# Scores and y on four 64x64 quadrants of TensorE, with keys and values put in order by their casts

## The chip, the cores and the metric

The kernel runs on one core of a Trainium2 chip. The metric is the device time of one execution in microseconds (us). Engines are named as the profile names them: PE is TensorE (PEld its weight loads), DVE is VectorE, ACT is ScalarE, POOL is GpSimd, SP is SyncE, whose queue issues most of the DMAs.

## The reference

Attention over 4 batches, 8 heads, 768 positions and head size 64, with 4 sink keys and a causal window of 128, followed by a feed-forward layer with a maximum of three products:

```python
scores = scale * np.matmul(q, k.transpose(0, 1, 3, 2))
rel = pos[:, None] - pos[None, :]
keep = (pos[None, :] < 4) | ((rel >= 0) & (rel < 128))
a = softmax(np.where(keep, scores, -1e9))            # over the keys
x = np.matmul(a, v)                                  # to (3072, 512)
h = np.maximum(np.maximum(x @ w1, x @ w2), x @ w3)   # (3072, 768)
out = h @ w_out                                      # (3072, 512), float32
```

## The kernel before

The 3072 positions are cut into 12 chunks of 256, three to a batch. Matrices are bf16, sums are float32 in PSUM. A chunk passes these steps:

- `load` brings q, k and v (512 KB each) in through SP's queue, into two buffers each. Row p of a tile holds positions 2p and 2p + 1, so that 512 bytes lie together.
- `cast_qk` (L95) and `cast_v` (L104) turn float32 into bf16. For q and k there are two casts per chunk, of 128 rows by 512 values. For v there are four, of 64 rows by 512, since they also move the rows to their places. After chunk 4, `cast` (L475) gives all of them to POOL, in the order k, q, v.
- Q and k are transposed: chunks 0 to 3 on PE (`turn`, L109), later ones by DMA (`turn_dma`, L150). Q takes one transfer, k takes two of 64 rows.
- `score` (L259) works head pair by head pair, four pairs to a chunk. The stationary operand is 64 partitions (the head's size) by 128 keys, and the two heads of a pair sit in the two row halves of the array. Keys and queries come in blocks of 128. A chunk with a predecessor in its batch has three steps: the previous chunk's last key block against the first query block, the chunk's first key block against both, its last key block against the second. These are 128, 256 and 128 columns. The first chunk of a batch (0, 3, 6, 9) has only the last two.
- `expo` on ACT takes the exponential, `mask` (L289) on DVE multiplies by a mask of ones and zeros (chunks 0 and part of 1 add theirs on PE first).
- `sink_score` (L294) gets the scores of the 4 sink keys for the second and third chunk of a batch. It reads `ks`, which `sink_k` (L224) copies on POOL out of the batch's first `kT`.
- `av_open` and `av` (L324, L339) multiply by v and divide by the sum of the weights, `xpose_dma` transposes the result.
- `ffn_h` (L383) makes h: 72 matmuls of 256 columns per chunk, a copy on ACT and two maxima on DVE for every two blocks.
- Y = h times w_out is made by `ffn_y` with full weights, or by `y_open`, `y_turn` and `y_out` (L428, the loop L431) in row halves: two turns of 12 matmuls of 512 columns, with the halves of a wave writing to different banks of PSUM. After the first turn a matmul of one column, the fence, is put in; its bank is given to the next score.

The order is written out by hand. Up to chunk 3 it is a list of calls (L486 to L692). Then a loop (L693) runs rounds: round i makes the scores, the weights and the A·V of chunk i + 1, h of chunk i and y of chunk i - 1, loads chunk i + 3, and casts and transposes chunk i + 2. Rounds 3, 10 and 11 have an order of their own, rounds 4 to 9 another. Every engine, and SP's queue, runs its instructions in the order of this list, so a waiting one holds up all behind it. Banks of PSUM are handed out in the order in which they are given back.

In the list, POOL's work ahead of the scores of chunk 4 is: mask factors (L592), casts of v of chunk 2, of q and k of chunk 3, three of v of chunk 3 (L651 to L654), one of k of chunk 4 (L659), four of v of chunk 4 (L662, L689 to L691), and then `sink_k` at the head of round 3.

Of the kernel before, what the change touches and what calls it, by code (L numbers as in the profile page):

```python
# [16 lines left out]
def kernel(  # L17
# [31 lines left out]
    with tc.manual_schedule():  # L49
# [16 lines left out]

        RING = 4
# [6 lines left out]
        raws, bfs = {}, {}  # L74

# [28 lines left out]
        def cast_v(ci, n, i, eng):  # L104
            eng.tensor_copy(  # L105
                vb[ci % RING][64 * i:64 * i + 64, n, :, 0:D],
                raws[ci, "v"][64 * n:64 * n + 64, :, i])

        def turn(ci, w, g, eng=None):  # L109
# [8 lines left out]
            if w == "q":  # L118
                f(  # L119
                    qT[ci % RING][:, 2 * g:2 * g + 2].rearrange("q p i n r -> q (p i) (n r)"), pt)  # L120
            else:
                f(
                    kT[ci % RING][:, :, 2 * g:2 * g + 2].rearrange("q n p i r -> q n (p i) r"),
                    pt.rearrange("q x (n r) -> q n x r", r=64))
# [25 lines left out]
        def turn_dma(ci, w):  # L150
            if ci >= NCH:
                return
            if w == "q":
                nc.sync.dma_start_transpose(
                    out=qT[ci % RING].rearrange("q p i n r -> q (p i) (n r)"),
                    in_=bfs[ci, w].rearrange("s p i a d -> s (p i a d)"))
                return
            for n in range(2):
                nc.sync.dma_start_transpose(
                    out=kT[ci % RING][:, n].rearrange("q p i r -> q (p i) r"),  # L160
                    in_=bfs[ci, w][64 * n:64 * n + 64].rearrange("q p i a d -> q (p i a d)"))


# [25 lines left out]
        msk0 = const.tile([128, 2, 3, 128], BF16, name="msk0")  # L189

# [20 lines left out]

        sel = const.tile([128, 2, 32], BF16, name="sel")

# [10 lines left out]
        def sink_k(b):  # L224
            x = kT[(b * CPB) % RING]
            for a in range(2):
# [3 lines left out]
                    x[hp, 0, :, :, 0:2].rearrange("q p i r -> q p r i"))  # L230
# [28 lines left out]
        def score(ci, pairs):  # L259
            b, c = divmod(ci, CPB)  # L260
# [20 lines left out]

        def expo(ci, p):
            lo = 0 if ci % CPB else 1
# [5 lines left out]
        def mask(ci, p, eng=None):  # L289
            lo = 0 if ci % CPB else 1  # L290
# [3 lines left out]
        def sink_score(ci):  # L294
# [4 lines left out]
            for p in range(NP):  # L299
                nc.tensor.matmul(  # L300
                    st[32 * p:32 * p + 32].rearrange("q n (i r) -> q n i r", i=2),
                    lhsT=ks[b % 2][:, p],
                    rhs=qT[ci % RING][:, p].rearrange("q i n r -> q n i r"),
# [6 lines left out]
        def sink_v(b):  # L310
# [3 lines left out]
            for a in range(2):  # L314
                for p in range(NP):
                    nc.tensor.matmul(
                        sv[32 * p:32 * p + 32, a], lhsT=sel[:, a], rhs=x[:, 0, 2 * p + a],
# [21 lines left out]
        def av(ci, p):  # L339
# [16 lines left out]
            if ci not in xs:  # L356
                xs[ci] = work.tile([128, 2, NP, 2, D], BF16, tag="x", bufs=2, name="x_sb")
            nc.vector.tensor_mul(xs[ci][:, :, p], o[:, :, :, 0:D],  # L358
# [5 lines left out]
        def xpose(ci, t, eng=None):  # L364
            eng = eng or nc.scalar
            if t == 0:
                xTs[ci] = work.tile([128, 2, DS, 128], BF16, tag="xT", bufs=3, name="xT")
            pt = bank([128, DS, 128], BF16, "xt")
            x = xs[ci][:, t].rearrange("q p a d -> q (p a d)")
            for ds in range(DS):  # L370
                nc.tensor.transpose(pt[:, ds], x[:, ds * 128:(ds + 1) * 128], ident)
            (nc.scalar.copy if eng is nc.scalar else eng.tensor_copy)(xTs[ci][:, t], pt)
            give(pt)

        def xpose_dma(ci, eng=None):
            xTs[ci] = work.tile([128, 2, DS, 128], BF16, tag="xT", bufs=3, name="xT")
            (eng or nc.sync).dma_start_transpose(
                out=xTs[ci].rearrange("q t s r -> q (t s) r"),
                in_=xs[ci].rearrange("q t p a d -> q (t p a d)"))
# [3 lines left out]
        def ffn_h(ci, fp, wi, cuts=1, eng=nc.scalar):  # L383
# [3 lines left out]
            for f in range(2):  # L387
                c0 = (2 * fp + f) * 128
                for ds in range(DS):
                    nc.tensor.matmul(  # L390
                        hp[:, f].rearrange("q (i t r) -> q i t r", i=2, t=2),
                        lhsT=w_sb[wi][:, ds, c0:c0 + 128],
# [459 lines left out]
```

## Time and profile before

| | |
|---|---|
| median of 3 runs | 176.93 us (176.87 to 177.23) |
| the profiled execution, its own time | 178.83 us |
| its span, first to last instruction | 177.1 us |
| granted clock of TensorE, mean | 1.000 |
| busy: PE, weight loads, DVE | 167.9, 128.2, 121.7 us |
| busy: ACT, POOL | 86.8, 65.9 us |

The share of an engine is an average over the whole span. Where a stage's limit lies is read from that stage: the busy time of each engine within a stretch, the order of instructions in time, and the idle time ahead of an instruction with what ended it. A line such as "L105 POOL CAST vb<-v_raw 64x512 bf16<-64x512 f32 x4" says which line of the kernel the instruction comes from, its engine, what it writes and reads, the partitions by elements, and how many are merged. The duration of a matmul includes its way through the array, so the distance between starts is what it costs in a stream.

### The profile page before, as it was taken

What the parts mean: (1) busy time and instruction counts of PE and PEld (TensorE: products, weight loads), DVE (VectorE), ACT (ScalarE), POOL (GpSimd) and SP (SyncE); (2) the same over time, 40 slices, a digit from 0 to 9 for tenths busy, and PEclk for the clock granted to TensorE, in tenths of its full rate; (3) what the DMA queues carried; (4) which work ended last, traced back from release to release, by engine and by line L of the source; (5) the groups of instructions that cost most, each with busy time, mean ns of one, the idle gap of its engine ahead of it and who ended that gap; (6) DMA issues with size and microseconds to landing.
All of it is one profiled execution on the core that took longest, in us unless ns stands there. A gap on an engine that the chain in (4) does not pass through costs nothing.

```text
span 177.1 us, 4816 instructions
## 1 busy us (share of the span) xinstructions
PE 167.9 (95%) x1956; PEld 128.2 (72%) x1961; DVE 121.7 (69%) x263; ACT 86.8 (49%) x174; POOL 65.9 (37%) x126
## 2 busy tenths in 40 slices
PE   7869988899999999999999999999999999999992
PEld 2436777676688588598698797697797796796871
DVE  3287763679599696677776775876776776876451
ACT  4588525477871931931823914914715716420210
POOL 7289605454685296056055046065073000000000
PEclk9999999999999999999999999999999999999999
DMA  5999999999999999799998999997999405303203
GB/s 144 298 282 181 161 223 236 222 288 276 277 197 302 289 229 237 172 301 171 229 262 214 230 217 234 183 273 194 255 210 226 73 15 162 122 0 63 118 2 118
DMA packets 70694, 34.91 MB, mean 197 GB/s; under 512 B 26640, under 2 KB 69136, under 8 KB 70672
## 3 DMA queue, kind: packets, MB, share of 16 engines
q1 hardware_dynamic: 64976, 31.33, 79.4%
q0 software_dynamic: 5552, 3.15, 12.9%
q8 instruction: 15, 0.25, 0.6%
q10 hardware_dynamic: 144, 0.13, 0.2%
q14 instruction: 7, 0.06, 0.1%
HBM read 25.17 MB, written 6.29 MB: 178 GB/s over the span
## 4 chain that ended last, share of the span: by engine, by line
PE 75%; DMA 11%; POOL 6%; DVE 5%; issue 2%; POOLq 0%; SPq 0%; DVEq 0%
PE h_ps L390 44%; PE y_ps L431 10%; DMA q_raw<-in_q_dram 7%; PE y_ps L411 6%; PE st L274 5%; PE o L350 5%; DMA v_raw<-in_v_dram 3%; POOL w L237 3%; DVE h_sb L401 2%; POOL vb L105 1%; PE o L332 1%; DVE e_sb L292 1%; PE y_ps L453 1%; DVE x_sb L358 1%; PE pt L115 1%
## 5 line engine op out<-in xcount | busy, mean ns | idle before, releaser
L390 PE MATMUL h_ps<-xT,w 128*128 128x256 bf16 x864 | 101.6, 273 | 0.9 <-DMA w<-in_moe_w_dram 0.8
L390 PEld LDWEIGHTS <-w 128*128 128x128 bf16 x864 | 81.6, 98 | 11.8 <-DMA w<-in_moe_w_dram 1.2
L401 DVE TENSOR_TENSOR h_sb<-h_sb,h_ps 128x512 bf16<-128x512 bf16 (+1 forms) x74 | 49.1, 670 | 19.7 <-PE h_ps L390 18.0
L286 ACT ACTIVATE e_sb<-st 128x512 bf16<-128x512 f32 (+1 forms) x96 | 45.9, 585 | 6.6 <-PE st L274 6.5
L397 ACT CAST h_sb<-h_ps 128x512 bf16<-128x512 f32 x35 | 20.6, 589 | 49.7 <-PE h_ps L390 49.6
L292 DVE TENSOR_TENSOR e_sb<-e_sb,msk 128x1024 bf16<-128x1024 bf16 (+1 forms) x42 | 28.0, 679 | 10.8 <-ACT e_sb L286 10.8
L105 POOL CAST vb<-v_raw 64x512 bf16<-64x512 f32 x42 | 27.8, 661 | 15.7 <-DMA v_raw<-in_v_dram 13.2
L101 POOL CAST k_bf<-k_raw 128x512 bf16<-128x512 f32 x18 | 11.0, 630 | 40.0 <-DMA k_raw<-in_k_dram 32.8
L358 DVE TENSOR_TENSOR x_sb<-o,rc 128x256 bf16<-128x256 f32 x48 | 20.4, 424 | 1.6
L431 PE MATMUL y_ps<-wo,h_sb 64*128 64x512 bf16 x168 | 20.7, 376 | 0.0
L350 PE MATMUL o<-vb,e_sb 128*128 128x65 bf16 x352 | 16.6, 193 | 0.8 <-ACT e_sb L286 0.8
L350 PEld LDWEIGHTS <-e_sb 128*128 128x128 bf16 x352 | 14.6, 97 | 3.2 <-ACT e_sb L286 1.0
L274 PE MATMUL st<-qT,kT 64*128 64x128 bf16 (+1 forms) x256 | 14.8, 237 | 0.2 <-DVE qT L119 0.2
L101 POOL CAST q_bf<-q_raw 128x512 bf16<-128x512 f32 x17 | 10.2, 619 | 9.0 <-DMA q_raw<-in_q_dram 9.0
L274 PEld LDWEIGHTS <-kT 64*128 64x128 bf16 x256 | 9.2, 94 | 5.6 <-issue 1.8
L431 PEld LDWEIGHTS <-h_sb 64*128 64x128 bf16 x168 | 8.9, 94 | 5.7
L411 PE MATMUL y_ps<-wo,h_sb 128*128 128x512 bf16 x49 | 12.6, 380 | 0.3
L355 DVE RECIPROCAL rc<-o 128x4 f32<-128x4 f32 x48 | 8.4, 174 | 3.6 <-PE o L350 3.6
L306 ACT ACTIVATE e_sink<-sk 128x256 bf16<-128x256 f32 x8 | 3.1, 389 | 13.3 <-PE sk L300 13.3
L411 PEld LDWEIGHTS <-h_sb 128*128 128x128 bf16 x54 | 4.9, 98 | 5.4 <-DVE h_sb L401 0.5
L237 POOL DMA_DIRECT2D w<-in_moe_w_dram x9 | 7.1, 790 | 0.0
L445 DVE COPY y_sb<-y_ps 128x512 f32<-128x512 f32 x8 | 5.4, 686 | 0.8 <-PE y_ps L431 0.5
(73 smaller groups left out, 87.3 us busy)
## 6 DMA issues: line engine op xcount, KB each, us to landing
k_raw<-in_k_dram SPq DMA_DIRECT2D x11, 512.0 KB, 5.5
v_raw<-in_v_dram SPq DMA_DIRECT2D x11, 512.0 KB, 7.5
out_dram<-y_sb SPq DMA_DIRECT2D x11, 512.0 KB, 3.1
q_raw<-in_q_dram SPq DMA_DIRECT2D x10, 512.0 KB, 7.2
w<-in_moe_w_dram POOLq DMA_DIRECT2D x9, 256.0 KB, 6.8
q_raw<-in_q_dram SPq DMA_DIRECT2D x4, 256.0 KB, 8.5
wo<-in_moe_w_out_dram POOLq DMA_DIRECT2D x2, 384.0 KB, 8.2
v_raw<-in_v_dram SPq DMA_DIRECT2D x2, 256.0 KB, 5.9
```

What stands on the lines that cost most here:

```text
L101: f(x[:, 2 * g:2 * g + 2].rearrange("q p i a d -> q p a i d"), y[:, 4 * g:4 * g + 4].rearrange("q (p a) i d -> q p a i d", a=2))
L105: eng.tensor_copy(vb[ci % RING][64 * i:64 * i + 64, n, :, 0:D], raws[ci, "v"][64 * n:64 * n + 64, :, i])
L274: nc.tensor.matmul(st[a][:, s:s + q1 - q0].rearrange("q n (i r) -> q n i r", i=2), lhsT=x[hp, n, p].rearrange("q i r -> q (i r)"), rhs=qc[ ...
L286: nc.scalar.activation(e[:, a, lo:], st[a][:, lo:], AF.Exp, scale=scale)
L292: (eng or nc.vector).tensor_mul(e[:, :, lo:], e[:, :, lo:], msk0 if lo else msk)
L350: nc.tensor.matmul(o[:, t, a], lhsT=e[:, a, s], rhs=vb[cv % RING][:, n, 2 * p + a], start=first, stop=True, skip_group_check=True)
L358: nc.vector.tensor_mul(xs[ci][:, :, p], o[:, :, :, 0:D], rc.unsqueeze(3).to_broadcast([128, 2, 2, D]))
L390: nc.tensor.matmul(hp[:, f].rearrange("q (i t r) -> q i t r", i=2, t=2), lhsT=w_sb[wi][:, ds, c0:c0 + 128], rhs=xTs[ci][:, :, ds].rearrang ...
L397: (nc.scalar.copy if eng is nc.scalar else eng.tensor_copy)(dst, hp)
L401: nc.vector.tensor_max(dst[:, x], dst[:, x], hp[:, x])
L411: nc.tensor.matmul(yp, lhsT=hs[ci][:, fb, t * 128:(t + 1) * 128], rhs=wo[:, fb], start=(fb == 0), stop=(fb == FB - 1))
L431: nc.tensor.matmul(yps[ci][t], lhsT=hs[ci][hp, fb, t * 128:(t + 1) * 128], rhs=wo[hp, fb], start=(turn == 0 and fb == 0), stop=(turn == 1 ...
```

## The change

From chunk 3 on (`NEW = 3`):

- Scores (`score4`) and y use four quadrants of 64 rows by 64 columns. Keys are put in order so that a block of 64 holds consecutive positions. For a chunk with a predecessor, the quadrants that the mask makes all zero are left out, and the rest is ordered in three steps of equal length in the two column halves: 192, 128 and 64 columns. The first chunk of a batch keeps 256 and 128. A wave of y has four matmuls instead of two, 24 to a turn.
- The exponentials of such a chunk then have 384 columns instead of 512 (`expo4`); `mask4` reads them with an overlapping pattern and writes a tile of the old form.
- `cast_k` puts the keys in order with eight casts of 32 rows, `cast_v` the values likewise. K is transposed by one transfer.
- POOL casts q first, then k, then v. For chunk 4, DVE makes four of k's casts and POOL four. `masks2` (L592's place) and `masks3` build the new masks and a second selector on POOL.
- The A·V result and its transpose have their middle dimensions exchanged. H reads its columns in runs of 32.
- In rounds 4 to 9 the first turn of y comes after one pair of scores instead of two, in round 10 likewise, and the fence stands a pair of scores further ahead of the score that takes its bank. In round 3, q is transposed ahead of k.

```diff
+        def cast_k(ci, n, h, i, eng):
...
+            x, y = 64 * h + 32 * i, 64 * n + 32 * h
+            f = eng.copy if eng is nc.scalar else eng.tensor_copy
+            f(bfs[ci, "k"][x:x + 32, :, n],
+              raws[ci, "k"][y:y + 32, :, i].rearrange("q (p a) d -> q p a d", a=2))
...
+            for h in range(2):
+                x, y = 64 * h + 32 * i, 64 * n + 32 * h
+                eng.tensor_copy(
+                    vb[ci % RING][x:x + 32, n, :, 0:D], raws[ci, "v"][y:y + 32, :, i])
...
-            for n in range(2):
-                nc.sync.dma_start_transpose(
-                    out=kT[ci % RING][:, n].rearrange("q p i r -> q (p i) r"),
-                    in_=bfs[ci, w][64 * n:64 * n + 64].rearrange("q p i a d -> q (p i a d)"))
+            nc.sync.dma_start_transpose(
+                out=dst, in_=bfs[ci, w].rearrange("s p i a d -> s (p i a d)"))
...
+        def masks2():
+            nc.gpsimd.memset(keep, 1.0)
+            for h in range(2):
+                for i in range(2):
+                    hp = slice(64 * h + 32 * i, 64 * h + 32 * i + 32)
+                    nc.gpsimd.affine_select(out=keep[hp, 0], in_=keep[hp, 0],
...
+                    nc.gpsimd.affine_select(out=keep[hp, 1], in_=keep[hp, 1],
...
+            nc.gpsimd.tensor_copy(msk0[:, :, 1:3], keep.unsqueeze(1).to_broadcast([128, 2, 2, 128]))
+            nc.gpsimd.tensor_copy(msk0[:, :, 0], keep[:, 1:2].to_broadcast([128, 2, 128]))
...
+        def masks3():
+            nc.gpsimd.tensor_copy(msk2, keep.unsqueeze(1).to_broadcast([128, 4, 2, 128]))
...
+        def score4(ci, pairs):
...
+            if c:
+                steps = (((kc, 0, 0, 3, 1), (kc, 0, 1, 4, 2)),
+                         ((kc, 1, 2, 4, 4), (kp, 1, 0, 2, 0)),
+                         ((kp, 1, 0, 1, 0), (kc, 1, 3, 4, 5)))
+            else:
+                steps = ((kc, 0, 0, 4, 0),) * 2, ((kc, 1, 2, 4, 4),) * 2
+            for p in pairs:
+                st = [bank([128, 6, 64], F32, "st") for a in range(2)]
+                for step in steps:
+                    for h in range(2):
+                        x, n, q0, q1, at = step[h]
+                        for a in range(2):
+                            hp = slice(64 * a, 64 * a + 64)
+                            nc.tensor.matmul(
+                                st[a][64 * h:64 * h + 64, at:at + q1 - q0]
+                                    .rearrange("q j (i r) -> q j i r", i=2),
+                                lhsT=x[hp, p, n, h],
...
+            for fb in range(FB):
+                for h in range(2):
+                    for a in range(2):
+                        t = a ^ turn
+                        hp = slice(64 * a, 64 * a + 64)
+                        c = t * 128 + 64 * h
+                        nc.tensor.matmul(
+                            yps[ci][t][64 * h:64 * h + 64], lhsT=hs[ci][hp, fb, c:c + 64],
+                            rhs=wo[hp, fb], start=(turn == 0 and fb == 0),
+                            stop=(turn == 1 and fb == FB - 1), skip_group_check=True)
...
-            for w in "kq":
-                for g in range(2):
-                    cast_qk(ci, w, g, q if q and w == "q" else nc.gpsimd)
+            for g in range(2):
+                cast_qk(ci, "q", g, nc.gpsimd)
+            for n in range(2):
+                for h in range(2):
+                    for i in range(2):
+                        cast_k(ci, n, h, i, nc.gpsimd)
...
-        factors(msk0, addm0)
+        masks2()
...
-        cast_qk(4, 'k', 0, nc.vector)
-        cast_qk(4, 'k', 1, nc.gpsimd)
+        for h in range(2):
+            for i in range(2):
+                cast_k(4, 0, h, i, nc.vector)
+                cast_k(4, 1, h, i, nc.gpsimd)
...
+        masks3()
...
                 score(n, (0,))
                 expo(n, 0)
-                score(n, (3,))
                 y_open(m)
                 y_turn(m, 0)
+                score(n, (3,))
                 expo(n, 3)
                 score(n, (1,))
```

150 lines of the change are left out of this document (110 added, 40 removed).

## The prediction

> **What bounds the kernel now.** I read the page first, then the rounds stretch by stretch, then one round on TensorE, then GpSimd's timeline where the change puts most of its new work.
>
> ```profile
> span 177.1 us, 4816 instructions
> PE 167.9 (95%) x1956; PEld 128.2 (72%) x1961; DVE 121.7 (69%) x263; ACT 86.8 (49%) x174; POOL 65.9 (37%) x126
> 95.86:109.02 13.16, 13.16 (x174) 10.78 (x173) 9.66 (x20) 6.57 (x13) 5.31 (x9) 1.00 1.14 230
> 109.02:122.04 13.02, 13.02 (x167) 10.21 (x167) 9.46 (x19) 6.57 (x13) 5.72 (x12) 1.00 1.02 211
> 122.04:134.30 12.26, 12.26 (x150) 9.63 (x149) 9.02 (x19) 5.52 (x12) 4.89 (x9) 1.00 1.05 237
> ```
>
> The last three lines are stretches, each a whole round of the loop: start:end, length, busy time of PE, weight loads, DVE, ACT, POOL, then the granted clock and the DMA share. In each, PE is busy for the whole length at clock 1.00, while POOL works 5 to 6 us. PE's instruction stream is the bound. A stall of PE is not made up later, and only what shortens PE's stream gains.
>
> One round on PE (start, length, what):
>
> ```profile
> 109.02 0.29 PE L300 MATMUL sk<-qT,ks 128*32 128x256 bf16 x4
> 109.25 0.62 PE L274 MATMUL st<-qT,kT 64*128 64x128 bf16 x12
> 109.70 1.46 PE L431 MATMUL y_ps<-wo,h_sb 64*128 64x512 bf16 x12
> 111.00 0.16 PE L437 MATMUL fence<-wo,h_sb 64*128 64x1 bf16 x1
> 111.03 0.62 PE L274 MATMUL st<-qT,kT 64*128 64x128 bf16 x11
> 111.47 1.47 PE L431 MATMUL y_ps<-wo,h_sb 64*128 64x512 bf16 x12
> L431 PE MATMUL y_ps<-wo,h_sb 64*128 64x512 bf16 x168 | 20.7, 376 | 0.0
> ```
>
> Twelve y matmuls run as six waves of two row halves. The last wave starts 1.46 - 0.376 = 1.08 us after the first, so a wave of 512 columns takes 0.217 us, 0.42 ns a column. The next start at 111.00 is 1.30 us on: six waves. Two pairs of scores take 109.70 - 109.25 = 0.45 us, 0.225 a pair, for 128 + 256 + 128 = 512 columns.
>
> **Scores and y on four tiles.** Where a chunk has a predecessor (4, 5, 7, 8, 10, 11), a pair's three steps stream 192 + 128 + 64 = 384 columns instead of 512. Saved: 128 x 0.42 = 0.054 us a pair, 0.216 a round. Chunks 3, 6, 9 stream 256 + 128 = 384 as before and save nothing. Y keeps its six waves of 512 columns per turn, now four matmuls in each instead of two: nothing saved, nothing added, if four quadrants run together as two halves do. What speaks for that are the four column strips of the sink values, and for the weight loads also the full-width A·V loads:
>
> ```profile
> 95.86 0.25 PE L316 MATMUL sv<-vb,sel 128*32 128x65 bf16 x8
> L316 PE MATMUL sv<-vb,sel x32: 191/198/204, 16.1 to 134.2; 128*32 128x65 bf16 x32
> 117.09 0.65 PE L350 MATMUL o<-vb,e_sb 128*128 128x65 bf16 x16
> L350 PE MATMUL o<-vb,e_sb 128*128 128x65 bf16 x352 | 16.6, 193 | 0.8 <-ACT e_sb L286 0.8
> ```
>
> Eight sink matmuls start within 0.25 - 0.20 = 0.05 us: two waves of four strips, so four 32-column weight loads and 65 columns fit into 0.04 us, side by side. Sixteen A·V matmuls start (0.65 - 0.19) / 15 = 0.03 us apart, each with a full load. A 64-column load of a quadrant is not shown. I bound it by nothing added (it hides like the full load) and by twice the strip's 0.04. It is hidden behind steps of 192 and 128 columns (0.080 and 0.053 us) or nearly, but the third step lasts 64 x 0.42 = 0.027, so a pair loses 0 to 0.05, a round 0 to 0.2. I take 0.1, as neither row is nearer.
>
> The Trainium skill speaks against this step: "TensorEngine Tiling (Array Packing)", Restrictions, says column tiling switches off the fast weight load, and "TensorE: Matmul & The Clock Gate", LDWEIGHTS, gives columns / 1.2 ns, an estimated 53 ns for 64 columns. By it 26 ns a pair are lost, 0.1 us a round, which is the middle taken here; no row of this profile has a 64-column load.
>
> The second group of scores takes 111.47 - 111.00 = 0.47, 0.02 more than the first: the fence stands closely ahead of the score that reuses its bank. The change puts a whole pair more in between; I book that 0.02. Against it: the exps of scores 3 and 1 now wait for the first y turn, and the A·V openings take the banks that they free.
>
> ```profile
> L286 ACT ACTIVATE e_sb<-st 128x512 bf16<-128x512 f32 x64 | 32.8, 626 | 1.9 <-PE st L274 1.9
> L286 ACT ACTIVATE e_sb<-st 128x384 bf16<-128x384 f32 x32 | 13.1, 502 | 4.6 <-PE st L274 4.6
> ```
>
> An exp falls from 32.8/64 = 0.51 to 13.1/32 = 0.41 us. The four exps of pairs 3 and 1 begin some 2.0 us into the round (sink scores 0.23, a pair 0.17, a turn 1.30, a pair 0.17, and an estimated 0.1 until the first starts) and end at 3.65; PE gets to its openings at 3.6 (two more pairs and the second turn). That costs 0 to 0.1 us in the four rounds (chunks 5, 7, 8, 10) with this order, 0.2 together.
>
> Sum on PE: 6 x (0.216 + 0.02 - 0.1) + 2 x 0.02 - 0.2 = 0.65 us gained, between 0 and 1.4.
>
> ```profile
> 117.58 4.53 PE L390 MATMUL h_ps<-xT,w 128*128 128x256 bf16 x40
> L390 PE MATMUL h_ps<-xT,w 128*128 128x256 bf16 x864 | 101.6, 273 | 0.9 <-DMA w<-in_moe_w_dram 0.8
> ```
>
> H's matmuls of chunks 3 to 11 will read runs of 32 columns instead of 64. Today they start (4.53 - 0.27) / 39 = 0.109 us apart, the price of 256 plain columns (256 x 0.42 = 0.108): runs of 64 cost nothing, and I take the same for 32. The masks read one tile and write another at the same size, and DVE has 3 us free a round.
>
> **GpSimd's casts.** K's two casts per chunk become eight of 32 rows by 512, v's four become eight. Rows of GpSimd:
>
> ```profile
> 102.28 1.17 POOL L101 CAST k_bf<-k_raw 128x512 bf16<-128x512 f32 x2 [5.21 <-DMA k_raw<-in_k_dram]
> 107.10 2.61 POOL L105 CAST vb<-v_raw 64x512 bf16<-64x512 f32 x4 [0.54 <-DMA v_raw<-in_v_dram]
> 60.70 3.71 POOL L105 CAST vb<-v_raw 64x512 bf16<-64x512 f32 x4 [4.96 <-DMA v_raw<-in_v_dram]
> 62.24 1.70 DVE L292 TENSOR_TENSOR e_sb<-e_sb,msk 128x1024 bf16<-128x1024 bf16 x2
> ```
>
> Casts of 128 and of 64 rows last the same: 0.58 and 0.65 us. So the row count sets nothing, and I take 0.66 for 32 rows (bounds 0.58, and 0.93 as beside masks). The last two rows show that casts and masks on DVE hold each other up: four casts took 1.1 us more there. A chunk needs 1.2 (q) + 16 x 0.66 + up to 1.1 + 0.14 (sink keys, every third) = 12.0 to 13.0 us, against rounds of 12.8 on average, 12.7 after the gain. GpSimd goes from a spare engine to one as long as PE. V is wanted a round later, k's transpose some 2.5 us later, so I take no stall from it in the steady rounds. K's one transpose replaces two:
>
> ```profile
> kT<-k_bf SPq DMA_TRANSPOSE x16, 5.3
> qT<-q_bf SPq DMA_TRANSPOSE x8, 3.9
> ```
>
> The same rows as q's should land like q's. Nothing waits for kT today (PE has no idle time in the rounds), so that is worth 0. At chunk 4 q's transpose goes ahead of k's on SP's queue; two stores and the loads of chunks 5 and 6 stand behind k's, which waits for its last cast until about 52 us.
>
> ```profile
> 53.41 1.08 SPq L459 DMA_DIRECT2D out_dram<-y_sb  x2
> ```
>
> Today the stores go out from 53.4 us on, so this costs nothing.
>
> **The start-up, where it should hurt.** GpSimd and DVE between chunks 2 and 4, and PE's reader:
>
> ```profile
> 31.06 1.07 POOL L210 TENSOR_SCALAR msk<-addm 128x384 bf16<-128x384 bf16 x2
> L195 POOL TENSOR_SCALAR_AFFINE_SELECT addm<-addm 64x128 bf16<-64x128 bf16 x2 | 0.6, 293 | 0.1
> 34.53 1.26 POOL L105 CAST vb<-v_raw 64x512 bf16<-64x512 f32 x2 [2.40 <-DMA v_raw<-in_v_dram]
> 42.22 0.41 PE L350 MATMUL o<-vb,e_sb 128*128 128x65 bf16 x8
> 44.27 1.93 POOL L105 CAST vb<-v_raw 64x512 bf16<-64x512 f32 x3
> 47.21 0.84 POOL L101 CAST k_bf<-k_raw 128x512 bf16<-128x512 f32 x1 [1.01 <-DMA k_raw<-in_k_dram]
> 48.98 0.77 POOL L105 CAST vb<-v_raw 64x512 bf16<-64x512 f32 x1 [0.93 <-DMA v_raw<-in_v_dram]
> 50.24 2.50 POOL L105 CAST vb<-v_raw 64x512 bf16<-64x512 f32 x3
> 52.69 0.71 POOL L228 COPY ks<-kT 64x16 bf16<-64x16 bf16 x2
> 47.15 0.43 DVE L101 CAST k_bf<-k_raw 128x512 bf16<-128x512 f32 x1
> 49.30 0.72 DVE L105 CAST vb<-v_raw 64x512 bf16<-64x512 f32 x1
> 50.22 0.69 DVE L401 TENSOR_TENSOR h_sb<-h_sb,h_ps 128x512 bf16<-128x512 bf16 x1 [0.20 <-PE h_ps L390]
> 56.96 0.28 PE L300 MATMUL sk<-qT,ks 128*32 128x256 bf16 x4
> ```
>
> The sink keys' copies end at 53.4, and the sink scores that read them start at 56.96: 3.5 us to spare. Ahead of them in GpSimd's queue 8 casts become 18, and a mask copy of 1024 columns comes in (twice the 0.53 of the msk row): 18 x 0.66 + 1.1 + 0.1 + copies of 0.43 to 0.71 = 13.6 us from 44.27, so 57.9. The casts beside masks and casts on DVE were 1.1 us longer than 0.61 each today; with three more DVE casts I add 1.2: 59.1 (57.6 with k at 0.58; 60 with 2 us of hold-ups). PE waits 59.1 - 56.96 = 2.1 us (0.7 to 3.0), with the scores, y and h of the round behind it in its queue. DVE's added casts (three of 0.43, one of 0.72) delay its maxima by up to 1 us at 50.2, and PE with them; that lies inside this wait, but stays if the wait is gone. The new mask making at 31 us takes near 4.8 instead of 1.1 us (eight selects of 0.29, and eight copies and memsets of 0.1 to 0.53). Chunk 2's v casts, from 34.5 today, then begin at 35.9, and PE reads them at 42.2: free.
>
> **Sum.** The profiled execution took 178.83 us with a span of 177.1; the runs' median is 176.93. Span: 177.1 - 0.65 + 2.1 = 178.5; its own time 180.3; the median moves by the same 1.45: **178.4**. With the bounds (1.4 gained and 0.7 waited, nothing gained and 3.0 waited) it is 176.2 to 179.9.
>
> **Rivals.**
> - *GpSimd is in time* (the faster side). Casts of 32 rows that touch different rows run side by side, or are shorter. The point is 18 casts in 11 us, 0.61 each with no hold-up, or any overlap. Then the sink keys are ready before 56.96, up to 0.5 us of DVE's lag stays, and the result is 176.93 - 0.65 + 0 to 0.5: 176.3, down to 175.6. Against it: v's casts alternate between row halves now and still follow each other every 0.66 us. The Trainium skill, "GPSIMD Engine Reference", Instruction dispatch, states the mechanism: each core serves its own 16 partitions and begins the next instruction when its share is done. Chance 0.24.
> - *GpSimd becomes the bound.* From 0.64 us a cast on, with the masks in the way, it is slower than PE's 12.7. At 0.72 a chunk takes 13.9: 1.2 x 7 chunks less 2.5 us of slack is 6 us on top: 184, and 181 at 0.68. For it: every cast then has a mask or cast on DVE beside it. Chance 0.15.
> - *The quadrants don't run together*, so the change doesn't do what it says: each of 14 y turns doubles (+1.3 us each), near 197. Against it stand the strips' waves. Chance 0.03.
>
> **How the numbers follow.** The forecast case has 0.58. A difference of 0.2% (0.35 us) is about what a measurement of this kernel tells from no change: 176.58 to 177.28. The forecast case falls below that with 0.05 of the whole and inside with 0.04; the first rival lies below it with 0.20, inside with 0.04. Faster 0.25, same 0.08, slower 0.67. The range 176.0 to 181.5 leaves out the third rival, the larger part of the second and the end of the first.
>
> **What would show it.** Right: in the timeline the sink keys' copies on POOL end near 59 and PE's weight load of the sink scores lists a wait for POOL of about 2 us; scores of chunk 4 on take 0.17 to 0.2 us a pair; POOL is busy about 11 to 13 us a round; y's turns stay at 1.3 us. Wrong: no PE idle time near 57 us (first rival); PE waits in every round for POOL, or for kT behind it (second); y turns of 2.6 us (third). A gain in rounds of chunk 6 or 9 beyond 0.1 us would show a saving that I have not seen.

## The result and the profile after

The changed kernel takes **181.66 us** (median of 6 runs, 181.24 to 182.62), the kernel before 177.19 us beside it (6 runs, 176.87 to 177.61). The ratio is 1.0262, with a 95% interval of 1.0228 to 1.0296: 4.5 us slower, where 1.45 was forecast and 181.5 was the end of the range.

The page of the changed kernel: its span, the busy time of each engine, the chain of work that ended last, and GpSimd's two costliest groups (the last columns of a group are busy time, mean ns of one, idle time ahead).

```profile
span 179.5 us, 5636 instructions
PE 167.7 (93%) x2321; PEld 128.8 (72%) x2321; DVE 130.1 (72%) x267; ACT 82.4 (46%) x174; POOL 129.8 (72%) x221
POOL 46%; PE 27%; DMA 18%; issue 4%; SPq 2%; ACT 1%; DVE 0%; POOLq 0%; DVEq 0%
L90 POOL CAST k_bf<-k_raw 32x512 bf16<-32x512 f32 x60 | 46.9, 782 | 2.3
L129 POOL CAST vb<-v_raw 32x512 bf16<-32x512 f32 x70 | 44.0, 629 | 3.3
```

PE works as long as before (167.7 against 167.9 us); POOL went from 65.9 to 129.8, and has the largest share of the chain.

To see where the time is lost I cut both runs at the same places of PE's stream: the first score of chunk 3, the head of round 3 (where the sink keys are read), the head of round 10, the end. Two answers of the view of stretches, first before, then after (start:end, length, then busy time of PE, weight loads, DVE, ACT, POOL, the granted clock).

```profile
47.21:56.89 9.68, 9.68 (x113) 8.15 (x113) 8.19 (x19) 5.44 (x12) 7.01 (x12) 1.00 1.21 263
56.89:147.37 90.48, 90.43 (x1119) 71.52 (x1119) 66.96 (x138) 44.29 (x90) 32.99 (x56) 1.00 1.02 211
147.37:177.06 29.69, 26.14 (x266) 20.06 (x267) 17.23 (x33) 8.22 (x16) 0.00 (x0) 1.00 0.22 75
```

```profile
45.39:58.51 13.12, 10.04 (x129) 8.12 (x128) 12.85 (x24) 5.44 (x12) 12.21 (x19) 1.00 1.17 264
58.51:150.04 91.53, 90.34 (x1415) 72.04 (x1414) 70.31 (x138) 40.60 (x90) 86.12 (x130) 1.00 0.98 196
150.04:179.54 29.50, 26.05 (x316) 20.15 (x315) 17.23 (x33) 7.52 (x16) 0.15 (x1) 1.00 0.26 86
```

From chunk 3's first score on it is 134.15 us instead of 129.85. Of these 4.30, the start has 13.12 - 9.68 = 3.44, rounds 3 to 9 have 91.53 - 90.48 = 1.05, the end -0.19. (Ahead of the cut the profiled execution of before was 1.8 us later; that is its own, other executions of the same code reach chunk 3 as early as the changed kernel.) All further stage lengths are read in this way.

The start in the timeline, DVE, then POOL, then PE (start, length, engine, line, what; in brackets the idle time ahead and what ended it).

```profile
44.54 1.50 DVE L118 CAST q_bf<-q_raw 128x512 bf16<-128x512 f32 x2
45.96 3.08 DVE L90 CAST k_bf<-k_raw 32x512 bf16<-32x512 f32 x4
49.07 0.85 DVE L375 TENSOR_TENSOR e_sb<-e_sb,msk 128x768 bf16<-128x768 bf16 x1
49.93 1.91 DVE L129 CAST vb<-v_raw 32x512 bf16<-32x512 f32 x2
52.48 1.43 DVE L375 TENSOR_TENSOR e_sb<-e_sb,msk 128x768 bf16<-128x768 bf16 x2
...
42.44 4.07 POOL L129 CAST vb<-v_raw 32x512 bf16<-32x512 f32 x6
46.57 2.94 POOL L90 CAST k_bf<-k_raw 32x512 bf16<-32x512 f32 x4
57.48 0.42 POOL L278 COPY ks<-kT 64x16 bf16<-64x16 bf16 x2
57.97 1.17 POOL L118 CAST q_bf<-q_raw 128x512 bf16<-128x512 f32 x2
...
53.09 0.54 PE L466 MATMUL o<-vb,e_sb 128*128 128x65 bf16 x12 [3.02 <-DVE e_sb L375]
53.47 2.13 PE L512 MATMUL h_ps<-xT,w 128*128 128x256 bf16 x16
...
58.59 0.28 PE L418 MATMUL sk<-qT,ks 128*32 128x256 bf16 x4
```

PE stands for 3.02 us ahead of chunk 3's A·V, for a mask that DVE makes after its new casts. Four casts of k take 3.08 / 4 = 0.77 us each beside POOL's, against 0.43 for the single one of 128 rows before. The sink scores, where I had put the wait, don't wait: POOL's copies end at 57.9, and PE gets there later.

The Trainium skill, "SBUF — State Buffer", Who interferes with whom, says that DVE and GpSimd share one pair of SBUF ports under an exclusive lock. The two rows of four casts agree in kind, both engines' casts being longer than alone. They don't agree in size: if each cast held the lock to its end, a DVE cast (0.43 for the one of 128 rows) and a POOL cast (eight in 5.20 us below, 0.65 each) would take an estimated 1.1 us in turn, but DVE's four took 3.08 us and POOL's four 2.94, side by side.

One steady chunk on POOL, and PE's waits in the rounds:

```profile
97.51 1.17 POOL L118 CAST q_bf<-q_raw 128x512 bf16<-128x512 f32 x2
98.63 6.80 POOL L90 CAST k_bf<-k_raw 32x512 bf16<-32x512 f32 x8
105.49 5.20 POOL L129 CAST vb<-v_raw 32x512 bf16<-32x512 f32 x8
110.75 1.17 POOL L118 CAST q_bf<-q_raw 128x512 bf16<-128x512 f32 x2
...
145.00 5.19 POOL L129 CAST vb<-v_raw 32x512 bf16<-32x512 f32 x8
```

```profile
89.08 1.91 PE L512 MATMUL h_ps<-xT,w 128*128 128x256 bf16 x16 [0.17 <-ACT e_sb L369]
111.56 0.36 PE L352 MATMUL st<-qT,kT 64*64 64x192 bf16 x12 [0.69 <-DMA kT<-k_bf]
137.11 0.29 PE L418 MATMUL sk<-qT,ks 128*32 128x256 bf16 x4 [0.15 <-POOL ks L278]
```

POOL goes from chunk to chunk without a pause, here in 110.75 - 97.51 = 13.24 us (13.1 to 13.2 in the other chunks), while rounds without a wait last 12.8 on average (13.00, 12.93 and 12.44 in `plain_all` below). It falls behind until PE waits for what it made, for keys through their transfer or for the sink keys. (The first of these rows has another cause, told below.)

### The profile page after: what moved, and what is told of

It reads as the page before. It is cut to its first block, busy times and chain, and to the rows that moved or that the text cites. A ratio compares the mean times of both kernels' runs of the same rounds, so it can differ in the third digit from the quotient of the medians.

```text
span 179.5 us, 5636 instructions
## 1 busy us (share of the span) xinstructions
PE 167.7 (93%) x2321; PEld 128.8 (72%) x2321; DVE 130.1 (72%) x267; ACT 82.4 (46%) x174; POOL 129.8 (72%) x221
## 4 chain that ended last, share of the span: by engine, by line
POOL 46%; PE 27%; DMA 18%; issue 4%; SPq 2%; ACT 1%; DVE 0%; POOLq 0%; DVEq 0%
POOL vb L129 19%; PE h_ps L512 16%; POOL k_bf L90 15%; DMA q_raw<-in_q_dram 15%; POOL q_bf L118 4%; PE y_ps L532 4%; DMA v_raw<-in_v_dram 3%; POOL w L287 3%; PE y_ps L555 3%; SPq L182 1%; PE o L466 1%; POOL vb L123 1%; PE st L352 1%; POOL ks L278 1%; PE y_ps L577 1%
## 5 line engine op out<-in xcount | busy, mean ns | idle before, releaser
L512 PEld LDWEIGHTS <-w 128*128 128x128 bf16 x864 | 81.8, 98 | 12.1 <-issue 1.5
L90 POOL CAST k_bf<-k_raw 32x512 bf16<-32x512 f32 x60 | 46.9, 782 | 2.3
L129 POOL CAST vb<-v_raw 32x512 bf16<-32x512 f32 x70 | 44.0, 629 | 3.3
L384 DVE TENSOR_TENSOR e_sb<-e_part,msk 128x1024 bf16<-128x1024 bf16 x24 | 19.6, 836 | 8.0 <-ACT e_part L369 8.0
L369 ACT ACTIVATE e_part<-st 128x384 bf16<-128x384 f32 x48 | 19.7, 504 | 3.6 <-PE st L352 3.6
L555 PE MATMUL y_ps<-wo,h_sb 64*64 64x512 bf16 x336 | 20.8, 376 | 0.0
L555 PEld LDWEIGHTS <-h_sb 64*64 64x64 bf16 x336 | 9.8, 107 | 4.7
L532 PE MATMUL y_ps<-wo,h_sb 128*128 128x512 bf16 x54 | 12.8, 380 | 0.0
L369 ACT ACTIVATE e_sb<-st 128x384 bf16<-128x384 f32 x24 | 10.0, 503 | 5.9 <-PE st L352 5.9
L393 ACT ACTIVATE e_sb<-st 128x512 bf16<-128x512 f32 (+1 forms) x24 | 11.6, 591 | 2.0 <-PE st L326 1.9
L375 DVE TENSOR_TENSOR e_sb<-e_sb,msk 128x768 bf16<-128x768 bf16 x12 | 8.3, 697 | 2.9 <-ACT e_sb L369 2.7
L352 PE MATMUL st<-qT,kT 64*64 64x128 bf16 (+3 forms) x384 | 9.6, 226 | 0.7 <-DMA kT<-k_bf 0.7
```

Source lines behind the costliest of these rows:

```text
L90: f(bfs[ci, "k"][x:x + 32, :, n], raws[ci, "k"][y:y + 32, :, i].rearrange("q (p a) d -> q p a d", a=2))
L129: eng.tensor_copy(vb[ci % RING][x:x + 32, n, :, 0:D], raws[ci, "v"][y:y + 32, :, i])
L352: nc.tensor.matmul(st[a][64 * h:64 * h + 64, at:at + q1 - q0] .rearrange("q j (i r) -> q j i r", i=2), lhsT=x[hp, p, n, h], rhs=qT[ci % RI ...
L369: nc.scalar.activation(dst, st[a], AF.Exp, scale=scale)
L384: nc.vector.tensor_mul(x.rearrange("q a (t s) c -> q (a t) s c", t=2), y, msk2)
L512: nc.tensor.matmul(hp[:, f].rearrange("q (i t r) -> q i t r", i=2, r=x.shape[3]), lhsT=w_sb[wi][:, ds, c0:c0 + 128], rhs=x, start=(ds == 0 ...
```

## The experiments

Two theories: **A**, GpSimd's casts are the loss, at the start (through DVE) and as the pace of the rounds; **B**, TensorE's own part, the quadrants and the order of the rounds. The times of before beside these kernels lie between 176.98 and 177.10 us.

**The casts alone undone**, in all chunks (`plain_all`), in chunks 3 and 4 (`plain_start`), from chunk 5 on (`plain_rounds`):

```diff
-            if ci < NEW:
+            if ci < NEW or True:        # plain_start: ci < 5; plain_rounds: ci > 4
                 eng.tensor_copy(vb[ci % RING][64 * i:64 * i + 64, n, :, 0:D],
...
-            for n in range(2):
-                for h in range(2):
-                    for i in range(2):
-                        cast_k(ci, n, h, i, nc.gpsimd)
+            for g in range(2):
+                cast_qk(ci, "k", g, nc.gpsimd)
```

> The changed kernel with the casts of k and v of all chunks as they were (two of 128 rows, four of 64; they no longer put keys and values in order, so keys and values stand in the wrong places of the window; all else stays). Theory A (GpSimd's casts cost the time: DVE's casts and masks held up beside them at chunk 3, then k's transposes and sink keys late in the rounds): all of the 4.5 us goes and the scores' saving shows, 176.5 (176.0 to 177.2). Rival B (the new order of the rounds and the quadrants cost it too, through exps that end later): 178 to 179. POOL busy falls from 129.8 to about 70 us in both.

> The changed kernel with the old casts for chunks 3 and 4 alone (their keys and values are not put in order). Theory A: the 3.0 us wait of PE for DVE ahead of chunk 3's A.V goes, the later waits (0.7 for kT of chunk 8, 0.3 for the sink keys of chunk 10) stay or shrink: 178.3 (177.5 to 179). Rival: GpSimd is the bound of the rounds anyway, 129.8 us busy, and the waits come back later: 180.5 or more.

> The changed kernel with the old casts from chunk 5 on (those keys and values are not put in order). Theory A: the 3.0 us at chunk 3 stay, the later waits of about 1.1 us go: 180.5 (180 to 181). Rival, GpSimd as the bound of the rounds: 178.

Measured: `plain_all` 177.28 us (ratio 1.0000, 0.9966 to 1.0033), `plain_start` 176.97 (0.9988, 0.9959 to 1.0018), `plain_rounds` 181.35 (1.0199, 1.0146 to 1.0252). All three lie outside the ranges expected: by 0.08 us, by 0.5 on the fast side, by 0.35 on the slow side (the clock, below). Stretches of the first and the last, start and rounds 3 to 9:

```profile
45.87:55.72 9.85, 9.85 (x130) 8.22 (x130) 8.55 (x19) 5.43 (x12) 7.71 (x13) 1.00 1.21 255
55.72:146.07 90.35, 90.01 (x1415) 71.95 (x1414) 67.13 (x138) 40.51 (x90) 32.09 (x56) 1.00 1.02 209
```

```profile
45.39:58.52 13.13, 10.05 (x131) 8.14 (x130) 12.86 (x24) 5.44 (x12) 12.22 (x19) 1.00 1.14 277
58.52:148.87 90.35, 90.01 (x1415) 71.96 (x1415) 67.57 (x138) 40.51 (x90) 34.74 (x60) 1.00 0.96 197
```

The casts are the whole loss. Without them the change brings 0.13 us in the rounds and 0.20 at the end, not the 0.65 expected, and loses 0.17 at the start. This is read from one profiled execution of each; the times of the runs (a ratio of 0.9966 to 1.0033) can't tell so small a gain from nothing. In `plain_rounds` the waits of the rounds are gone and the start's 3.4 us stay. `plain_start` is the surprise: its rounds keep all the new casts and don't wait, though POOL has as much to do there. Its queue is only further ahead of PE (this is called its lead below): the first cast for chunk 5 begins 3.4 us ahead of the head of round 3 (51.88, 55.29), in the changed kernel 0.5 us ahead (57.97, 58.51). At the end of the queue the difference is 6.4 us, of which PE's earlier rounds are a part:

```profile
138.63 5.62 POOL L129 CAST vb<-v_raw 32x512 bf16<-32x512 f32 x8
```

These are the last value casts, which begin at 145.00 in the changed kernel. A queue slower than PE costs nothing as long as its lead lasts.

**Y on quadrants alone**, in the kernel before:

```diff
-                for a in range(2):
-                    ...
-                    nc.tensor.matmul(yps[ci][t], lhsT=hs[ci][hp, fb, t * 128:(t + 1) * 128], ...
+                for h in range(2):
+                    for a in range(2):
+                        ...
+                        c = t * 128 + 64 * h
+                        nc.tensor.matmul(yps[ci][t][64 * h:64 * h + 64], lhsT=hs[ci][hp, fb, c:c + 64], ...
```

> The kernel before with only y's turns on four quadrants (its scores, order and casts stay; the fence stays a half-array matmul). Theory A: four quadrants stream 512 columns in the time of two halves, but scores in row halves and y in quadrants now change the array's tiling three more times a round, each 0.09 us as at the sink scores (last h to first sink score 0.20 against 0.11): 7 x 0.3 = 2 us more, 179. Rival, quadrants run in pairs only: each turn doubles, 195. Rival, a change from halves to quadrants costs nothing: 177.2.

179.2 us, 1.0123 (1.0073 to 1.0172), as expected. A round on PE:

```profile
108.45 0.75 PE L274 MATMUL st<-qT,kT 64*128 64x128 bf16 x12
109.12 1.49 PE L433 MATMUL y_ps<-wo,h_sb 64*64 64x512 bf16 x24
...
110.55 0.63 PE L274 MATMUL st<-qT,kT 64*128 64x128 bf16 x12
111.11 1.49 PE L433 MATMUL y_ps<-wo,h_sb 64*64 64x512 bf16 x24
```

The two pairs ahead of y now take 109.12 - 108.45 = 0.67 us instead of 0.45, the turn 1.43 instead of 1.30, the next two pairs 0.56 instead of 0.47: each passage between row halves and quadrants costs some 0.08 to 0.15 us (there are three more a round; this round is 13.47 us long instead of 13.02, the ones around it 13.41 instead of 13.16 and 12.48 instead of 12.16). The 12.16 is the round that the prediction shows as 122.04:134.30; the next one begins at 134.20. So scores and y have to change form together. The Trainium skill, "TensorEngine Tiling (Array Packing)", Key Properties, says that a change of tiling mode drains the array. The row agrees, and gives a size.

**DVE's four casts as one of 128 rows** (`dve_one`), and with that the sink keys' copies ahead of the mask copy (`dve_one_sink`):

```diff
         for h in range(2):
             for i in range(2):
-                cast_k(4, 0, h, i, nc.vector)
                 cast_k(4, 1, h, i, nc.gpsimd)
+        nc.vector.tensor_copy(bfs[4, "k"][:, :, 0], raws[4, "k"][:, :, 0].rearrange(...))
...
+        sink_k(1)                       # dve_one_sink
         masks3()
```

> The changed kernel with DVE's four casts of 32 rows for chunk 4's keys made one of 128 rows (those keys are not put in order); GpSimd keeps all its casts. Theory A (DVE's casts each wait for a cast on GpSimd, 0.77 us instead of 0.43, and chunk 3's first mask stands behind them): PE's 3.0 us wait at chunk 3's A.V shrinks to about 1. But the sink keys still end 12.5 us after chunk 3's first score on GpSimd, and PE would read them 10 to 11 us after it: a wait of 1.5 to 2.5 takes its place. Time 180.5 to 181.3. Rival, DVE's casts are the whole of it: 178.8.

> The same, and the copies of the sink keys for chunk 4 put ahead of the mask copy and chunk 4's v casts in GpSimd's order. Theory A: the wait that took the other's place goes too; what is left of the start is about 1 us of DVE behind GpSimd (its q and v casts), and the rounds start earlier against GpSimd: 178.3 (177.6 to 179.3). Rival, the sink keys were never in the way: the same as without this step.

`dve_one`: 181.11 us, 1.0223 (1.0195 to 1.025), as expected. Its rows, one of DVE and two of PE:

```profile
46.46 0.83 DVE L788 CAST k_bf<-k_raw 128x512 bf16<-128x512 f32 x1
51.72 0.54 PE L466 MATMUL o<-vb,e_sb 128*128 128x65 bf16 x12 [1.27 <-DVE e_sb L375]
57.90 0.29 PE L418 MATMUL sk<-qT,ks 128*32 128x256 bf16 x4 [0.51 <-POOL ks L278]
```

The cast of 128 rows takes 0.83 us here, beside POOL's four, and not 0.43: so a DVE cast is longer for standing beside POOL's, and not for its 32 rows. The wait for DVE shrinks, and the wait for the sink keys that I had forecast appears behind it. `dve_one_sink`: 181.04 us, 1.0229 (1.0199 to 1.0258), a miss by 2.7. The stretches:

```profile
46.49:56.74 10.25, 9.88 (x129) 8.15 (x128) 9.97 (x21) 5.45 (x12) 9.46 (x16) 1.00 1.21 261
56.74:150.73 93.99, 90.49 (x1414) 72.04 (x1414) 71.02 (x138) 40.70 (x90) 88.43 (x133) 1.00 0.95 199
```

The start is 2.87 us shorter, and the rounds are 2.46 longer with the same work on PE (90.5 us). PE's waits there, in total, times, longest:

```profile
PE st L352 <- DMA kT<-k_bf: 2.1, 2, 1.8
PE sk L418 <- POOL ks L278: 1.0, 2, 0.8
```

What PE gains at the start it waits for later, since POOL's queue is hardly earlier: chunk 5's q casts start 12.1 us behind chunk 3's first score (58.55 - 46.49), 12.6 in the changed kernel (57.97 - 45.39).

**The change from chunk 6 on alone**, its round order kept (`new6`) or that of before (`new6_old`), with the start of before:

```diff
-        NEW = 3
+        NEW = 6
...
                 score(n, (0,))
                 expo(n, 0)
+                score(n, (3,))          # new6_old: the order of before
                 y_open(m)
                 y_turn(m, 0)
-                score(n, (3,))
```

> The whole change begun three chunks later (NEW = 6, the start of batch 2): chunks 3 to 5 as in the kernel before, new masks made on GpSimd after chunk 5's casts, y in quadrants from the round that makes chunk 6's scores on; the order of the rounds is the changed one. Theory A: the start costs nothing any more; rounds with chunks 7, 8, 10, 11 save 0.1 to 0.2 each, those of chunks 6 and 9 lose 0.27 each by the order: 177.0 (176.7 to 177.4). Rival, GpSimd with 16 casts holds up the rounds: 178 or more.

> The same with the order of rounds 4 to 9 of the kernel before (two pairs of scores ahead of the first turn of y). Theory: the 0.27 in the rounds of chunks 6 and 9 is PE waiting for exps that start later in the changed order (h's first bank waits for the last exp), and the A.V openings wait 0.1 for the same: both go. 176.2 (175.9 to 176.6), faster than both kernels. Rival, the loss is in the quadrants: no difference between the two orders.

178.68 us (1.0089, 1.0061 to 1.0118) and 179.0 (1.0103, 1.0078 to 1.0127): both missed, by 1.7 and 2.8. With the start untouched, the rounds wait instead. The new masks are made on POOL behind chunk 5's casts here, which takes it from 62.52 to 69.07 and so takes up to 6.5 us of its lead; no run has them elsewhere. PE's waits in `new6_old`, for the sink keys in rounds 6 and 9:

```profile
95.39 0.29 PE L425 MATMUL sk<-qT,ks 128*32 128x256 bf16 x4 [1.20 <-POOL ks L285]
135.10 0.29 PE L425 MATMUL sk<-qT,ks 128*32 128x256 bf16 x4 [1.17 <-POOL ks L285]
```

What did hold: in the order of before, the rounds that make the scores of chunks 6 and 9 last 12.2 us, in the new order 12.4. The row at 89.08 of the changed kernel shows why: the exps of such a chunk start later, and H's matmuls wait 0.17 us for a bank of theirs; the rest of the difference is not shown by a wait.

**Half of the value casts on ScalarE.** This takes four casts a chunk off GpSimd and gives them to ScalarE, which is idle for some 3 us between two copies of h; all else stays. Four kernels: the changed one (`v_act`), that with the start of `dve_one_sink` (`v_act_start`), the same in the order of before (`v_act_start_old`), and `new6_old` (`new6_old_act`).

```diff
-            for n in range(2):
+            for n in range(1 if 6 <= ci < NCH else 2):
                 for i in range(2):
                     cast_v(ci, n, i, nc.gpsimd)
...
                 ffn_h(i, 0, 1)
+                i + 2 < NCH and cast_v(i + 2, 1, 0, nc.scalar)
...
+                i + 2 < NCH and cast_v(i + 2, 1, 1, nc.scalar)
                 ffn_h(i, 0, 2)
```

> The changed kernel, with four of the eight value casts of chunks 6 to 11 (those of one half) given from GpSimd to ScalarE, in its idle time between two copies of h; the rest as changed. Theory A (GpSimd is the bound of the rounds, 13.2 us a chunk against rounds of 12.8): GpSimd falls to about 10.6 us a chunk, the waits of rounds 7 and 9 (0.7 and 0.2 us and what follows them) go, the 3.4 us at the start stay: 180.6 us (180.2 to 181.0), 1.0 less than the changed kernel. Rival B (the transfers, not the casts, are late): no change, 181.6. Rival C (ScalarE's casts delay the exps and the copies of h behind them): 182 or more.

> The same four value casts on ScalarE, and the start eased as before (one DVE cast of 128 rows for chunk 4's keys, the sink keys' copies of chunk 4 ahead of the mask copy). That start alone brought nothing (181.04), since the waits came back in rounds 4, 6, 7 and 9. Theory A (GpSimd's pace): with the pace eased those waits stay away, so that the start's gain is kept: the start 0.6 us longer than before's, the rounds 0.3 shorter: 177.4 us (177.0 to 178.2). Rival B (PE's other waits, whatever GpSimd's load, hold the rounds): about 180.5.

> The kernel with the value casts on ScalarE and the eased start, in the round order of before. If GpSimd's pace is eased and the rounds of chunks 6 and 9 lose the 0.3 us that the changed order costs each: 176.9 us (176.5 to 177.5), 0.5 less than the same in the changed order. If the order of before leaves score tiles waiting for banks, as the change's order was perhaps meant to spare: more than the same in the changed order, 178.

> The change from chunk 6 on alone, in the round order of before (179.0 us, rounds 6 and 9 of 14.3 us each), with the same four value casts on ScalarE. Theory A (GpSimd's pace): rounds 6 and 9 fall to 13.0 us, in all 2.6 us less: 176.4 us (176.0 to 177.0), 0.4 to 0.8 under the kernel before. Rival B (the order of before with the new score tiles holds the two rounds): 179.0 again.

| kernel | us | ratio and interval |
|---|---|---|
| `v_act` | 182.4 | 1.0303 (1.0265 to 1.0342) |
| `v_act_start` | 180.06 | 1.0171 (1.013 to 1.0212) |
| `v_act_start_old` | 179.43 | 1.0151 (1.0104 to 1.0199) |
| `new6_old_act` | 176.93 | 1.0003 (0.9976 to 1.003) |

`new6_old_act` is the clear case, inside the range expected though level with the kernel before and not faster: 2.1 us less than `new6_old`, rounds 3 to 9 in 90.79 instead of 93.06, no wait for the sink keys, and POOL now waits for its loads, here in round 7:

```profile
116.45 1.17 POOL L118 CAST q_bf<-q_raw 128x512 bf16<-128x512 f32 x2 [2.78 <-DMA q_raw<-in_q_dram]
```

`v_act_start` and `v_act_start_old` missed by 2.7 and 2.5. The order of before is 0.6 us better, where 0.5 was expected, but the runs overlap (179.37 to 181.11, 179.07 to 181.02). `dve_one_sink` had four waits in its rounds; `v_act_start` has two (2.00 and 0.42 us), `v_act_start_old` has one. The one that stayed is in round 5:

```profile
72.66 6.50 POOL L90 CAST k_bf<-k_raw 32x512 bf16<-32x512 f32 x8
...
84.60 0.36 PE L352 MATMUL st<-qT,kT 64*64 64x256 bf16 x8 [2.00 <-DMA kT<-k_bf]
```

These keys, chunk 6's, were cast until 79.16, and 5.4 us later (the median time of such a transfer in the changed kernel) they are there. ScalarE's casts come behind them in the queue and can't help. `v_act` missed altogether. Its rounds are 0.46 us shorter than the changed kernel's (91.07 against 91.53), but its start is 14.58 long:

```profile
53.30 0.54 PE L466 MATMUL o<-vb,e_sb 128*128 128x65 bf16 x12 [3.04 <-DVE e_sb L375]
53.67 3.39 PE L512 MATMUL h_ps<-xT,w 128*128 128x256 bf16 x16
```

```profile
53.30:57.40 4.10, 4.10 (x36) 3.13 (x37) 3.51 (x8) 0.29 (x1) 3.85 (x6) 0.58 1.03 300
```

The same 16 matmuls take 2.13 us in the changed kernel's profile (its row at 53.47), after a wait of 3.02. Here, after 3.04, the mean granted clock was 0.58 for 4 us (the number ahead of the last two).

**The wait filled with matmuls** (`v_act_warm`), to see whether the wait brings the clock down; and **four value casts of chunk 5 too on ScalarE** (`v_act3_start_old`), to take 2.6 us off POOL's queue ahead of chunk 6's keys; and the two orders mixed:

```diff
+        warm(12)                        # v_act_warm
         av(3, 0)
...
-            for n in range(1 if 6 <= ci < NCH else 2):
+            for n in range(1 if 5 <= ci < NCH else 2):      # v_act3_start_old
...
+                n % CPB or score(n, (3,))                   # new6_mixed_act
                 y_open(m)
                 y_turn(m, 0)
+                n % CPB and score(n, (3,))
```

> The changed kernel with four value casts a chunk on ScalarE (182.4 us, mean granted clock 0.987 to 0.991 in five of six runs), and twelve matmuls of zeros on 128x512 (2.6 us, results unused) put ahead of the A.V of chunk 3, into the 3.0 us in which TensorE waits there for the masks. Theory A (the wait itself makes the chip grant a lower clock behind it: in the profiled run the 16 matmuls after it took 3.39 us instead of 2.13, the granted clock 0.59 there): TensorE stays busy, the mean clock is 0.995 or more in all runs, and the time falls by what the clock took: 181.0 us (180.7 to 181.4). Rival B (the clock falls for another reason): 182.4 again, clock about 0.99. Rival C (the added matmuls end later than the masks): 183 or more.

> The kernel with the eased start, the order of before and four value casts a chunk on ScalarE (179.43 us, one wait of 2.0 us left, for the keys of chunk 6 in round 5), with four value casts of chunk 5 too on ScalarE, so that GpSimd comes to the keys of chunk 6 2.6 us earlier. Theory A (that wait is the rest of GpSimd's backlog from the start): it goes whole, 177.4 us (177.0 to 177.9). Rival B (the transfer of these keys is late by itself): 179.4 again.

> The change from chunk 6 on alone with four value casts a chunk on ScalarE (176.93 us in the order of before), the changed order only in the rounds whose chunk has a chunk before it (13.0 us there instead of 13.16), the order of before for chunks 6 and 9 (12.2 us instead of 12.4). If the orders' times add up as measured: 0.4 us less, 176.6 us (176.3 to 176.9), the best of all; if the two orders disturb one another: 177 or more.

`v_act_warm`: the mean granted clock is 0.997 to 1.000 in all six runs, so the wait did bring it down. The time was missed: it is 182.55 us all the same (1.0299, 1.0248 to 1.0349). The rows:

```profile
50.68 2.75 PE L197 MATMUL warm<-wz 128*128 128x512 bf16 x11
53.86 0.54 PE L466 MATMUL o<-vb,e_sb 128*128 128x65 bf16 x12 [0.43 <-DVE e_sb L375]
55.34 1.91 PE L512 MATMUL h_ps<-xT,w 128*128 128x256 bf16 x16 [0.94 <-DVE h_sb L522]
113.23 0.36 PE L352 MATMUL st<-qT,kT 64*64 64x192 bf16 x12 [0.79 <-DMA kT<-k_bf]
```

H's next matmuls wait 0.94 us for a maximum on DVE, probably since the fill took a bank of PSUM out of its turn (not tested), and the wait for chunk 8's keys is back. So the clock's price in the end time is not settled by this run.

`v_act3_start_old`: **177.32 us**, 1.0007 (0.9985 to 1.0029), where 177.4 was expected. Rounds 3 to 9:

```profile
55.60:146.25 90.65, 90.01 (x1415) 71.94 (x1415) 71.51 (x138) 58.10 (x118) 70.26 (x105) 1.00 1.01 206
```

The 2.0 us in round 5 went whole. A wait of 0.59 us stays (at 133.57, for chunk 10's keys), which GpSimd's casts don't explain: they had ended at 122.22, 11.3 us before. In `v_act_warm`, too, the casts of chunk 8's keys had ended at 100.76, 12.5 us before PE could start. There the transfer is late, not the cast: it takes up to 8.5 us from issue to landing in these two kernels and 6.1 at most in the changed one. Why is not tested. This kernel has the change's scores, y and ordered keys from chunk 3 on, and is level with before. `new6_mixed_act`: 176.89 us, 0.9998 (0.997 to 1.0026), against 176.6 expected; its 0.04 less than `new6_old_act` can't be told from nothing. No version beat the kernel before.

## Why the prediction was wrong

The direction and the cause's name were right (GpSimd's casts, and the start above all). Two steps failed, and the gain was half.

- **"DVE's added casts ... delay its maxima by up to 1 us at 50.2, and PE with them; that lies inside this wait".** This is the step that failed at the start. I took DVE's casts at 0.43 and 0.72, from rows in which POOL made single casts with pauses of 1.01 and 0.93 us ahead of them, and looked only at the sink keys. With POOL casting beside them the q casts took 0.75 each, the k casts 0.77, the v casts 0.96, and a mask behind them held the A·V for 3.02 us: 3.44 us at the start instead of 2.1. My own rows (v's casts beside masks, 3.71 us instead of 2.61) showed the hold-up; I used it for POOL alone and not for DVE.
- **The wait for the sink keys** (59.1, a wait of 0.7 to 3.0): this was near, and was covered by the other wait. The profiled execution of before reaches chunk 3's first score 1.8 us later, so the times are counted from there: the copies were forecast to end after 59.1 - 47.21 = 11.9 us and ended after 57.9 - 45.39 = 12.5. PE had read them after 56.96 - 47.21 = 9.75 us before, so that they alone would have cost 2.8 us. `dve_one`, with a shorter wait ahead, brought out 0.51 us of it.
- **"I take no stall from it in the steady rounds."** This step failed in the rounds: I had 12.0 to 13.0 us a chunk, and the one shown took 13.24: 1.17 for q, 6.80 for k, 5.20 for v, and the gaps between. The price of a cast was near (0.65 alone, 0.66 forecast), but eight beside masks took 6.80, that is 0.85 each, 1.6 us on top instead of "up to 1.1". And I counted 2.5 us of slack for keys that have 5.4 us of transfer behind them. The second rival described this with chance 0.15. That its 181 to 184 holds the result is luck: it put 2.6 to 6 us on top of the forecast in the rounds, where 1.19 were found, and the rest came from the start. (Its 181 doesn't follow from its own sum either: at 0.68 us a cast a chunk takes 13.3 us, and 0.6 x 7 - 2.5 = 1.7 gives 180.1.)
- **The gain on PE**, 0.65 (0 to 1.4): 0.33 without the casts, by `plain_all` against before, rounds and end. In `plain_all` three pairs in a row take 0.51 us (109.46 to 109.97), 0.17 each as forecast before the loss for weights, so that the 64-column loads are hidden; the y turn ahead of them lasts 1.30 us (108.12 to 109.42) as before. Each of the two rounds of chunks 6 and 9 loses 0.27 (12.44 against 12.17 before), 0.23 of it by the new order (12.21 in `new6_old`), where I had booked a gain of 0.02, and the others lose some of their saving at the A·V openings (0.35 us there instead of 0.22, from 111.36 to 111.71). The Trainium skill's price of a 64-column load without fast load ("TensorE: Matmul & The Clock Gate", LDWEIGHTS) would make a pair an estimated 0.20; the trace doesn't agree.
- **The clock** was in no step. In the changed kernel five of six runs had a mean granted clock of 0.981 to 0.991, the profiled one 1.000; before lies at 0.996 or more. The kernels with the 3 us wait showed it (`plain_rounds` too: 179.97 and 180.07 us in the runs at 0.999 and 0.998, 181.29 to 181.64 and once 183.65 at 0.989 to 0.991), and no other did but for single runs.
- **Right**: k's one transfer costs nothing in itself (it doesn't land like q's, in 3.9 us, as I had it, but in 5.4, about as the two did before, 5.3), the masks at 31 us are free (their making took 5.7 us, not 4.8), casts on different rows don't run side by side (the fast rival, 0.24), and the quadrants run together (197, 0.03).

In sum, forecast +2.1 - 0.65 = +1.45; the stretches gave +3.44 at the start, +0.86 from round 3 to the end, of which 1.19 are waits and their followers and -0.33 the gain. What the clock took is on top, some 0.4 us by the median of the runs against the one run at full clock (181.66, 181.24).

What stays open is how much of the clock's loss the end time feels, since rounds that wait for GpSimd take up a later PE. Two figures bound it: the start of `v_act` is 14.58 - 13.12 = 1.46 us longer than that of the changed kernel at full clock, and in `plain_rounds`, whose rounds don't wait, three of the runs at the lower clock took 1.2 to 1.7 us more than the two at full clock.

## What to carry to other kernels

An engine that is given work must be counted as a queue with a lead: from where it is busy without a gap, work per round against the round, and how much lead it brings. A lead hides a queue that is too slow, and a stall mended at the front comes back behind as long as the queue is not shortened (181.66, 181.04, 180.06, 179.43, 177.32 us as the mends were added one by one). Casts that are cut into pieces by rows cost as many whole casts, and DVE and GpSimd must be priced beside each other, from rows in which both work.

## What the runs showed of the hardware

- DVE and GpSimd, casting at the same time: DVE 0.77 instead of 0.43 us (0.83 for a cast of 128 rows, `dve_one`), GpSimd's four 2.94 us, (2.94 - 0.61) / 3 = 0.78 apart, instead of 0.65; beside masks 0.85 a cast.
- After 3.02 to 3.04 us without work on TensorE, its clock fell to about half in some executions and not in others: matmuls of 256 columns 0.213 us apart instead of 0.109, for 3.3 us (`v_act`). With such a wait 14 of 18 runs had a mean clock of 0.991 or less (the changed kernel, `plain_rounds`, `v_act`); with a longest wait of 1.8 to 2.0 us it was 2 of 18 (`dve_one_sink`, `v_act_start`, `v_act_start_old`). The Trainium skill, "TensorE: Matmul & The Clock Gate", Why this matters for your kernels, warns of gaps beyond some 3 us. The runs agree in the main.
- A passage between row halves and quadrants costs TensorE some 0.08 to 0.15 us (`y_alone`).
